# Keys and queries of the first unit: from the evicted tiles to their score buffers on chip, and the second weights asked for two tiles later

## The chip, the cores and the metric

One core of a Trainium2 chip. The metric is the device time of the whole kernel in microseconds (us), the median over several executions. Profiles are of single executions; times inside them are us from the span's start.

## The reference

Two attention blocks share one input x (2048 x 448, 16 heads of 28) and are mixed by a gate per row. A looks at 8 keys, two rows apart, at and behind each query; B at all keys.

```python
def _B_ref(x, wqkv, wo):
    qkv = (x @ wqkv).reshape(B, S, 3, H, Dh).transpose(2, 0, 3, 1, 4)
    q, k, v = qkv[0], qkv[1], qkv[2]
    scores = einsum("bhqd,bhkd->bhqk", q, k) * (Dh ** -0.5)
    o = einsum("bhqk,bhkd->bhqd", softmax(scores), v)
    return o.transpose(0, 2, 1, 3).reshape(B, S, D) @ wo
...
g = sigmoid((x * gate_w).sum(-1, keepdims=True))
return g * _A_ref(x, A_wqkv, A_wo) + (1 - g) * _B_ref(x, B_wqkv, B_wo)
```

## The kernel before

The kernel works in three stages. The first, up to about 259 us, projects x to the queries and keys (Q, K) and values of B and A. The second runs B's attention in 16 units of four heads (a group, four groups) and 512 queries, beside A's attention on GpSimd. The third multiplies by the output weights. To keep float32 accuracy on products of rounded operands, an operand is split into a high part (a rounding copy, on ScalarE, ACT) and a low part (a subtraction, on VectorE, DVE, or GpSimd, POOL), and a product is the sum of three.

Everything here is in the first stage. Its loop (from line 449 on: `for n, t in enumerate(tiles)`) goes over output tiles n; a Q or K tile is 128 rows (four heads and a bit) by 512 columns (a block nb of four). The first tiles in order are, as block and part: 0: K block 0; 1: Q block 0; 2: the third part of block 0; 3: K block 1; 4 and 5: block 1's others; 6: K block 2; 7: K block 3; 8 to 11: the rest of the first weight set. From tile 12 on the second weight set is used. The scores of unit 0 read the K rows of group 0 (`rows[0][0] == D` in the change) and the Q rows of block 0.

Order of one round n (the engines run their instructions in the order in which they are written): loads of weights that are due (`load_w`, line 244), the split of weights that are due (`split_w`, line 267: for the second set two quarters at n = 8 and two at n = 9; copies on ACT in line 212, subtractions on POOL in line 213), the split of an x block (at n = 0, 3, 5), the tile's products on TensorE (PE), then `qk_tile` (line 337). That evicts the tile from PSUM: for n < 10 (`FULL`) a copy on ACT into `hi` (line 341) and a subtraction on DVE into `lo` (line 342), and `qk_store` (line 329) puts both into the DRAM tensors qk_hi and qk_lo. `hi` and `lo` of one tile are the halves of one buffer of a pool of eight (`pp`). Whole tiles use the PSUM buffers PS[n % 4]; from n = 10 on (`project_halves`, line 308) each tile is computed in two halves of the contraction at a time, in PJ = PS[0:2], with 21 products a tile, and is summed on POOL.

From tile 11 on (`S1_START`) score products of the first pass, which finds the maxima, are mixed in between: four a tile (`s1_half`, line 153; the product itself is line 143 in `s1_mm`), which read a K block kc from KH[0] and 128 columns of QP[0]. KH[i] holds the four heads of a group at partitions 0, 32, 64 and 96, 28 rows each. QP[i] is a pair of buffers with every second head, and zeros in the other rows.

All loads and stores of this stage but the first x block's go through the queue of SyncE (SP), which issues them in the order written; a transfer that has to wait holds those behind it. `dma_r` (line 100) issues one transfer and stands for all of KH's, QP's and the stores'; `load_w` issues lines 256 (raw, three quarters of the contraction, two column ranges for the second set) and 218 (wt, the tail, twice, for each of two ranges). `load_k` (line 103) reads a group's K back from qk_hi in four transfers, one a head, `load_qhi` (line 130) a unit's Q. Before the loop SP has issued the first weights and all of x.

In before, the loop's end issues the second weights behind tiles 2 (raw) and 3 (tail), Q of unit 0 behind tile 3, and K of group 0 in two column ranges behind tiles 7 and 8.

Of the kernel before, what the change touches and what calls it, by code (L numbers as in the profile page):

```python
# [15 lines left out]
S, D, H, DH = 2048, 448, 16, 28  # L16
# [9 lines left out]
def gated_mix_kernel(ctx: ExitStack, tc: tile.TileContext, xT, xn, gw, wA, wB, woAB, out):  # L26
# [4 lines left out]
    qk_hi = dram.tile([2 * D, S], F32R, name="qk_hi")  # L31
# [40 lines left out]
    KH = [cp.tile([128, S], F32R, name=f"KH{i}") for i in range(2)]  # L72
# [5 lines left out]
    QP = [[cp.tile([128, 512], F32R, name=f"QP{i}{k}") for k in range(2)] for i in range(2)]  # L78
# [6 lines left out]
    def pair(name):  # L85
        return pp.tile([128, 2, 512], F32, tag="P", name=name)
# [3 lines left out]
    def ptile(name):  # L90
        if name[0] == "w":
            return pair(name)[:, 0, :]
        h = half.setdefault(name[:2], [])
        if not h:
            t = pair(name)
            h.extend((t[:, 1, :], t[:, 0, :]))
        return h.pop()

    def dma_r(dst, src):
        nc.sync.dma_start(dst.bitcast(F32), src.bitcast(F32))  # L100


    def load_k(g, t, src, c=slice(0, S)):
        for h in range(4):
            r = D + 112 * g + DH * h
            dma_r(t[32 * h:32 * h + DH, c], src[r:r + DH, c])
# [18 lines left out]
    qhis = {}  # L125
# [4 lines left out]
    def load_qhi(u):  # L130
        g, b = divmod(u, NB)
        qhis[u] = QP[u % 2]
        for h in range(4):
            r = 112 * g + DH * h
            dma_r(qhis[u][h % 2][32 * h:32 * h + DH, :], qk_hi[r:r + DH, 512 * b:512 * b + 512])
# [46 lines left out]
    def max_turn(t):  # L182
        r = sp.tile([128, 32], F32, name="nms")
        nc.vector.transpose(r, t)
        return r
# [18 lines left out]
    with tc.tile_pool(name="xp", bufs=1) as xp, tc.tile_pool(name="wp", bufs=2) as wp:  # L204
# [3 lines left out]
        def raw3():  # L208
            return wp.tile([128, 3, 450], F32, tag="raw", name="raw", bufs=2)
# [6 lines left out]
        def both(dst, src, eng=nc.sync):  # L216
            for h in (0, 64):
                eng.dma_start(dst[h:h + 64], src)
# [25 lines left out]
        def load_w(wi, tails=(False, True)):  # L244
            src, cols = WSRC[wi]
            if wi not in wraw:
                wraw[wi] = raw3(), wp.tile([128, 450], F32, tag="wt", name="wt"), sum(c1 - c0 for c0, c1 in cols) + 2 * (wi == GATE)
            r, t, _ = wraw[wi]
            for tail in tails:
                o = 0  # L250
                for c0, c1 in cols:
                    e = o + c1 - c0
                    if tail:
                        both(t[:, o:e], src[384:448, c0:c1])
                    else:
                        nc.sync.dma_start(r[:, :, o:e], src[0:384, c0:c1].rearrange("(k p) c -> p k c", p=128))
                    o = e

                if wi == GATE:
                    if tail:  # L260
                        both(t[:, o:o + 2], gw[0:2, 384:448].rearrange("i p -> p i"))
                    else:
                        for kt in range(3):
                            nc.sync.dma_start(r[:, kt, o:o + 2],
                                              gw[0:2, 128 * kt:128 * kt + 128].rearrange("i p -> p i"))

        def split_w(wi, kts):
            if wi not in wsets:
                wsets[wi] = [wp.tile([128, 4, 450], F32R, tag=g, name=f"{g}{wi}") for g in ("wh", "wl")]
            wh, wl = wsets[wi]  # L270
            r, t, n = wraw[wi]
            for kt in kts:
                split(wh[:, kt, :n], wl[:, kt, :n], r[:, kt, :n] if kt < 3 else t[:, :n], nc.gpsimd)
# [55 lines left out]
        def qk_store(nb, rows, hi, lo):  # L329
            cs = slice(512 * nb, 512 * nb + 512)  # L330
            for dst, t in ((qk_hi, hi), (qk_lo, lo)):
                o = 0
                for r0, r1 in rows:
                    dma_r(dst[r0:r1, cs], t[o:o + r1 - r0])
                    o += r1 - r0

        def qk_tile(n, nb, rows):
            hi, lo = ptile("qkh").bitcast(F32R), ptile("qkl").bitcast(F32R)
            if n < FULL:
                bank = PS[n % 4][:, 0, :]  # L340
                nc.scalar.activation(hi, bank, AF.Copy)
                nc.vector.tensor_tensor(out=lo, in0=bank, in1=hi.bitcast(F32), op=ALU.subtract)
                qk_store(nb, rows, hi, lo)
                return
            raw = pair("raw")
            nc.scalar.activation(raw, PJ[n % 2], AF.Copy)
            r = raw[:, 0, :]
            nc.gpsimd.tensor_tensor(out=r, in0=r, in1=raw[:, 1, :], op=ALU.add)

            def finish():  # L350
                nc.scalar.activation(hi, r, AF.Copy)
                nc.gpsimd.tensor_tensor(out=lo, in0=r, in1=hi.bitcast(F32), op=ALU.subtract)
                qk_store(nb, rows, hi, lo)

            fini.append((n + 1, finish))
# [52 lines left out]
        r, t = xst[:, 0, 0:3, :], xst[:, 0, 3, :]  # L408
# [16 lines left out]
        def split_third():  # L425
            c = slice(256, 384)
            for kt in range(3):
                split(wh0[:, kt, c], wl0[:, kt, c], wr1[:, kt, 128:256])
            split(wh0[:, 3, c], wl0[:, 3, c], wt0[:, c])
# [19 lines left out]
        for n, t in enumerate(tiles):  # L449
            wi = t[0]  # L450
            for w in loads:
                if loads[w] == n:
                    load_w(w)
            for w in splits:
                i, k = (n - splits[w][0]) * splits[w][1], splits[w][1]
                if 0 <= i < 4:
                    split_w(w, range(i, i + k))
            if n == 0:
                split_third()
            if n in (3, 5):  # L460
                split_x((n + 1) // 2)
            if n < FULL:
                project(n)
            else:
                project_halves(n, [S1_START <= m < S1_START + 80 for m in (n, n + 1)])
            if t[1] == "qk":
                qk_tile(n, t[2], t[3])
            elif t[1] == "v":
                add_halves(n, V[:, t[2], :, 0:DH])
            else:  # L470
                a_tile(n, t[2], t[3])
            if n == 0:
                split_x(1)
            while fini and fini[0][0] <= n:
                fini.pop(0)[1]()
            if n in (2, 3):
                load_w(1, (n == 3,))
            if n == 3:
                load_qhi(0)
            if n == 7:  # L480
                load_k(0, KH[0], qk_hi, slice(0, 1536))
            if n == 8:
                load_k(0, KH[0], qk_hi, slice(1536, S))
            if n == 16:
                for i in (1, 2):
                    nc.sync.dma_start(a_scr[i][:, 0:NJ, :].rearrange("c j e -> c (j e)").rearrange(
                        "c (a b) -> c a b", b=NJ), omg[0:8, None, :].to_broadcast([8, 56, NJ]))
            if n == 32:
                nc.gpsimd.memset(V[:, :, :, DH:], 1.0)
            if n == 22:  # L490
                load_k(1, KH[1], qk_hi)
            if n == 62:
                load_k(0, KL[0], qk_lo)
            if parts and parts[0][0] <= n:
                _, u, t = parts.pop(0)
                max_store(u, max_turn(t.bitcast(F32)))
            if finished and n < len(tiles) - 3:
                u = finished.pop(0)
                parts.append((n + 3, u, max_parts(u)))
            if n == 64:  # L500
                gate = []
                for sgn, dst in ((-1.0, g_t), (1.0, omg)):
                    e = sp.tile([128, NJ], F32, name="ez")
                    nc.scalar.activation(e, zt, AF.Exp, scale=sgn)
                    nc.gpsimd.tensor_tensor(out=e, in0=e, in1=V[:, 0, :, DH], op=ALU.add)
                    gate.append((dst, e))
            if n in (66, 68):
                nc.vector.reciprocal(*gate.pop(0))
            if n == 70:
                r = max_turn(omw)  # L510
                for a in range(4):
                    nc.sync.dma_start(og_scr.rearrange("(j p) -> j p", j=NJ)[:, 32 * a:32 * a + 32],
                                      r[32 * a:32 * a + NJ, :])
            if n == 76:
                load_q(0)
# [167 lines left out]
    for c in range(8):  # L683
# [20 lines left out]
        n = 0  # L704
# [197 lines left out]
    for u in range(NU - 1):  # L902
        f = NJ * (u + 1)
# [239 lines left out]
```

## Time and profile before

| | |
|---|---|
| median of 3 executions | 927.08 us (926.46 to 927.43) |
| the profiled execution | 927.55 us |
| its span, first to last instruction | 925.1 us |
| mean granted clock of TensorE | 0.996 |
| PE, DVE, ACT, POOL busy | 914.6, 732.6, 652.8, 620.9 us |

The page lists busy times by engine over the whole span. For a change of a few lines at the beginning, the answers of the trace for the first 60 us are what is to be read: what each engine did in order of time, what it waited for, and the clock that PE was granted. Transfers are listed by the time that SP took to issue them, which is not the time that they took to land. A granted clock of 1.00 is 2.4 GHz, of 0.50 is 1.2 GHz.

### The profile page before, as it was taken

The numbers are of one execution on the slowest core, as the hardware profiler recorded it, in microseconds if no ns is written. First come the engines' busy times: TensorE is split into PE (matmuls) and PEld (weight loads), VectorE is DVE, ScalarE is ACT, GpSimd is POOL, SyncE is SP. The second block draws the span as 40 slices with busy tenths as digits, with TensorE's granted clock in tenths as the row PEclk, the third lists the DMA queues.
The fourth block names the chain that finished last, engine by engine and source line by source line (L and its number), as shares of the span: only waits on it lengthen the run. The fifth ranks groups of instructions, "written<-read, shape, count | busy, mean of one in ns | idle before, by whom it ended". The sixth has DMA issues, their size and how long they took to land.

```text
span 925.1 us, 21392 instructions
## 1 busy us (share of the span) xinstructions
PE 914.6 (99%) x8396; PEld 541.3 (59%) x8396; DVE 732.6 (79%) x977; ACT 652.8 (71%) x802; POOL 620.9 (67%) x485
## 2 busy tenths in 40 slices
PE   9899999999999999999999999999999999999998
PEld 6688999999954444444444444444444444466667
DVE  6388999999979999999999999999998888500012
ACT  6346534343378888888888888888989889855551
POOL 2289856464469799999999999999994851300100
PEclk9899999999999999999999999999999999999999
DMA  9867603444362341335135232421412123553422
GB/s 254 283 191 219 185 11 82 130 121 128 104 240 64 99 123 46 88 103 130 41 96 151 85 101 63 139 74 30 107 42 53 33 60 99 149 156 112 137 83 98
DMA packets 101124, 104.34 MB, mean 113 GB/s; under 512 B 61652, under 2 KB 71252, under 8 KB 100240
## 3 DMA queue, kind: packets, MB, share of 16 engines
q1 hardware_dynamic: 100880, 102.72, 39.2%
q8 instruction: 65, 1.06, 0.5%
q10 hardware_dynamic: 144, 0.26, 0.2%
q14 instruction: 35, 0.29, 0.1%
HBM read 61.99 MB, written 40.48 MB: 111 GB/s over the span
## 4 chain that ended last, share of the span: by engine, by line
PE 94%; DMA 2%; ACT 1%; SPq 1%; issue 0%; DVE 0%; POOL 0%; ACTq 0%; DVEq 0%; POOLq 0%
PE T L1011 30%; PE av L973 26%; PE r L296 15%; PE T L812 8%; PE r L291 7%; PE r L143 4%; PE T L143 4%; ACT P L1014 1%; PE T L790 1%; DMA V<-in_xT 1%; DMA onlo<-on_lo 1%; DMA qk_hi<-qkh 0%; DMA KH<-qk_hi 0%; SPq L100 0%; SPq L851 0%
## 5 line engine op out<-in xcount | busy, mean ns | idle before, releaser
L1014 ACT ACTIVATE P<-T 128x1024 f32<-128x1024 f32 x512 | 497.1, 1024 | 89.5 <-PE T L1011 87.6
L147 DVE TENSOR_REDUCE MX<-T 128x1 f32<-128x512 f32 x470 | 443.4, 954 | 39.6 <-PE T L143 15.7
L973 PE MATMUL av<-P,V 128*32 128x512 f32 x2048 | 272.8, 605 | 0.0
L1011 PEld LDWEIGHTS T<-QH,KH 30*128 30x128 f32 x1024 | 90.9, 181 | 228.9 <-ACT P L1014 198.5
L143 PE MATMUL T<-KH,QP 28*128 28x512 f32 x704 | 222.0, 461 | 0.1
L1011 PE MATMUL T<-QH,KH 30*128 30x512 f32 x1024 | 220.6, 491 | 1.4 <-ACT P L1014 1.3
L160 DVE TENSOR_REDUCE MX<-r 128x2 f32<-128x1024 f32 x160 | 192.5, 1221 | 29.4 <-PE r L143 24.7
L1011 PE MATMUL T<-QH,KL 28*128 28x512 f32 x1024 | 189.0, 393 | 0.0
L1011 PE MATMUL T<-QL,KH 28*128 28x512 f32 x1024 | 187.4, 392 | 0.0
L608 POOL TENSOR_TENSOR prod<-qt,kt 128x896 f32<-128x896 f32 x64 | 135.1, 2115 | 4.7 <-DMA kt<-a_scr 4.7
L360 ACT ACTIVATE raw<-r 128x896 f32<-128x896 f32 (+1 forms) x64 | 58.9, 921 | 96.7 <-PE r L296 96.7
L663 POOL TENSOR_TENSOR oat<-oat,prod 128x896 f32<-128x896 f32 x56 | 118.1, 2109 | 2.4
L143 PE MATMUL r<-KH,QP 64*128 64x512 f32 x320 | 99.4, 395 | 3.3 <-DMA KH<-qk_hi 3.2
L143 PEld LDWEIGHTS T<-KH,QP 28*128 28x128 f32 x704 | 86.0, 181 | 23.7 <-ACT P L1014 13.9
L658 POOL TENSOR_TENSOR prod<-vt,L 128x896 f32<-128x896 f32 x56 | 95.5, 1705 | 0.5
L361 POOL TENSOR_TENSOR ast<-raw 128x448 f32<-128x448 f32 x48 | 55.5, 1156 | 57.8 <-ACT raw L360 49.2
L1011 PEld LDWEIGHTS T<-QL,KH 28*128 28x128 f32 x1024 | 92.5, 184 | 0.0
L1011 PEld LDWEIGHTS T<-QH,KL 28*128 28x128 f32 x1024 | 91.8, 183 | 0.9
L296 PE MATMUL r<-wh,xh 64*128 64x448 f32 (+1 forms) x512 | 87.8, 363 | 0.0
L973 PEld LDWEIGHTS av<-P,V 128*32 128x32 f32 x2048 | 40.3, 108 | 78.9 <-issue 73.9
L800 DVE TENSOR_TENSOR oalo<-T,oah 128x384 fp32r<-128x384 f32 x16 | 8.9, 557 | 90.9 <-ACT onhi L799 82.3
L296 PE MATMUL r<-wh,xl 64*128 64x448 f32 (+1 forms) x384 | 70.9, 363 | 0.0
(110 smaller groups left out, 1158.5 us busy)
## 6 DMA issues: line engine op xcount, KB each, us to landing
a_scr<-ast SPq DMA_DIRECT2D x24, 448.0 KB
qk_hi<-qkh SPq DMA_DIRECT2D x24, 256.0 KB
qk_lo<-qkh SPq DMA_DIRECT2D x24, 256.0 KB
rbc<-rs SPq DMA_DIRECT2D x60, 64.0 KB
QP<-qk_hi SPq DMA_DIRECT2D x64, 56.0 KB
KL<-qk_lo SPq DMA_DIRECT2D x16, 224.0 KB
QH<-qk_hi SPq DMA_DIRECT2D x64, 56.0 KB
QL<-qk_lo SPq DMA_DIRECT2D x64, 56.0 KB
```

The lines of the kernel that those rows point to most:

```text
L143: nc.tensor.matmul(bank, qhis[u][h % 2][r, 128 * qs:128 * qs + 128], KH[u // NB % 3][r, 512 * kc:512 * kc + 512], start=True, stop=True)
L147: nc.vector.tensor_reduce(MX[:, n % NMX:n % NMX + k], bank, axis=X, op=ALU.max)
L160: nc.vector.tensor_reduce(m, PM[k], axis=X, op=ALU.max)
L291: nc.tensor.matmul(bank, ws[c][rows, k, t[4]:t[4] + 128], x, start=first, stop=last)
L296: nc.tensor.matmul(bank[:, 0:cols], x, ws[c][rows, k, 0:cols], start=first, stop=last)
L608: nc.gpsimd.tensor_tensor(out=p, in0=qt[c], in1=kvt["k", c % 2][:, HALO - DIL * w:HALO - DIL * w + NJ, :], op=ALU.mult)
L658: nc.gpsimd.tensor_tensor(out=dst.rearrange("p j (h d) -> p j h d", d=DH), in0=kvt["v", c % 2][:, HALO - DIL * w:HALO - DIL * w + NJ, :].r ...
L663: nc.gpsimd.tensor_tensor(out=oat[c], in0=oat[c], in1=oat[c, w], op=ALU.add)
L812: writes(bank, nc.tensor.matmul(bank[:, :D], src, wo[c][:, k, :], start=(first and k == ks[0] and i == 0), stop=(last and k == ks[-1] and ...
L973: nc.tensor.matmul(av[32 * h:32 * h + 32, :], V[:, kt, 4 * g + h, :], tiles_[h], start=(kt == 0), stop=(kt == NJ - 1), skip_group_check=True)
L1011: nc.tensor.matmul(bank[a], (KH[g % 3], KH[g % 3], KL[g % 2])[t][r, ks], (qh, ql, qh)[t][r, :], start=(t == 0), stop=(t == 2))
L1014: nc.scalar.activation(p, RP[0] if a == "2" else mine, AF.Exp, scale=SCALE)
```

## The change

When a K tile of group 0 (tiles 0, 3, 6, 7) has been copied to `hi` on ACT, SP issues four transfers, one a head, from `hi` straight into KH[0], ahead of the tile's two stores. Likewise four into QP[0] for the Q tile of block 0 (tile 1). The loads of KH[0] (group 0) and QP[0] (unit 0) from qk_hi are gone; everything is still stored into qk_hi and qk_lo. The second weights are asked for behind tiles 4 and 5 instead of 2 and 3; their splits stay at tiles 8 and 9.

```diff
@@ qk_tile
             if n < FULL:
                 bank = PS[n % 4][:, 0, :]
                 nc.scalar.activation(hi, bank, AF.Copy)
+                for h in range(4):
+                    r, f = slice(32 * h, 32 * h + DH), slice(DH * h, DH * h + DH)
+                    if rows[0][0] == D:
+                        dma_r(KH[0][r, 512 * nb:512 * nb + 512], hi[f])
+                    elif rows[0][0] == 0 and nb == 0:
+                        dma_r(QP[0][h % 2][r], hi[f])
                 nc.vector.tensor_tensor(out=lo, in0=bank, in1=hi.bitcast(F32), op=ALU.subtract)
                 qk_store(nb, rows, hi, lo)
                 return
@@ the loop over tiles
-            if n in (2, 3):
-                load_w(1, (n == 3,))
+            if n in (4, 5):
+                load_w(1, (n == 5,))
             if n == 3:
-                load_qhi(0)
-            if n == 7:
-                load_k(0, KH[0], qk_hi, slice(0, 1536))
-            if n == 8:
-                load_k(0, KH[0], qk_hi, slice(1536, S))
+                qhis[0] = QP[0]
```

## Rows read from the trace of the kernel before

**Rows 1.** The page: span, and part 1, each engine's busy time, share, instructions.

```profile
span 925.1 us, 21392 instructions
...
PE 914.6 (99%) x8396; PEld 541.3 (59%) x8396; DVE 732.6 (79%) x977; ACT 652.8 (71%) x802; POOL 620.9 (67%) x485
```

**Rows 2.** Chain of waits, 0 to 130 us: start, duration, what the chain ran through.

```profile
9.86 21.22 PE r L291 x90
...
32.33 4.03 DMA qk_hi<-qkh
...
36.79 3.77 DMA KH<-qk_hi
```

**Rows 3.** PE in order of time: start, duration, operation, idle time before and its releaser.

```profile
33.54 1.20 PE L291 MATMUL r<-xh,wh 64*128 64x512 f32 x8
...
37.10 0.41 PE L291 MATMUL r<-xh,wl 64*128 64x512 f32 x2
40.70 0.76 PE L143 MATMUL r<-KH,QP 64*128 64x512 f32 x1 [3.18 <-DMA KH<-qk_hi]
...
41.97 0.76 PE L143 MATMUL r<-KH,QP 64*128 64x512 f32 x1
```

**Rows 4.** Busy time by stretch: PE, PEld, DVE, ACT, POOL (x instructions), granted clock, DMA, GB/s.

```profile
37.50:40.00 2.50, 0.01 (x1) 0.00 (x0) 0.00 (x0) 0.00 (x0) 1.26 (x1) 1.00 0.87 225
40.00:46.80 6.80, 6.02 (x26) 4.63 (x27) 2.64 (x3) 1.48 (x2) 0.37 (x1) 0.50 0.73 235
46.80:60.00 13.20, 13.20 (x116) 10.84 (x114) 10.72 (x9) 6.25 (x9) 11.00 (x9) 1.00 0.53 180
```

**Rows 5.** SP's queue in order of time, 0 to 60 us: start, duration, line, transfer.

```profile
18.23 0.32 SPq L100 DMA_DIRECT2D qk_hi<-qkh  x1
...
20.71 2.08 SPq L256 DMA_DIRECT2D raw<-in_wB  x2
...
28.34 2.00 SPq L100 DMA_DIRECT2D QP<-qk_hi  x4
30.45 0.35 SPq L100 DMA_DIRECT2D qk_hi<-qkh  x1
30.89 0.38 SPq L100 DMA_DIRECT2D qk_lo<-qkh  x1
...
32.33 0.76 SPq L100 DMA_DIRECT2D qk_hi<-qkh  x1
...
36.41 2.31 SPq L100 DMA_DIRECT2D KH<-qk_hi  x4
...
49.85 1.17 SPq L218 DMA_DIRECT2D wt<-in_wB  x2
```

**Rows 6.** Line 100's transfers: duration min/median/max in ns, first and last start.

```profile
L100 SPq DMA_DIRECT2D onhi<-onhi x4: 746/770/881, 908.6 to 911.2; - x4
L100 SPq DMA_DIRECT2D onlo<-onlo x4: 746/747/754, 912.0 to 914.4; - x4
```

**Rows 7.** SP's queue in order of time, 895 to 925 us.

```profile
908.60 3.32 SPq L100 DMA_DIRECT2D onhi<-onhi  x4
912.01 3.13 SPq L100 DMA_DIRECT2D onlo<-onlo  x4
```

**Rows 8.** ACT in order of time, 9 to 42 us.

```profile
18.19 1.68 ACT L212 ACTIVATE xh<-V 128x512 fp32r<-128x512 f32 x3 [1.74 <-DMA V<-in_xT]
...
22.41 1.68 ACT L212 ACTIVATE xh<-V 128x512 fp32r<-128x512 f32 x3
...
29.12 0.93 ACT L212 ACTIVATE wh<-raw 128x384 fp32r<-128x384 f32 x2
31.11 0.60 ACT L341 ACTIVATE qkh<-r 128x512 fp32r<-128x512 f32 x1 [1.06 <-PE r L291]
```

**Rows 9.** SP's waits, 0 to 60 us: who waited for what, us, times, longest.

```profile
SPq L256 <- DMA V<-in_xT: 2.1, 2, 1.3
```

**Rows 10.** DVE in order of time, 27 to 47 us.

```profile
31.73 0.69 DVE L342 TENSOR_TENSOR qkh<-r,qkh 128x512 fp32r<-128x512 f32 x1 [1.79 <-DMA QP<-qk_hi]
```

**Rows 11.** Busy time by stretch, 31.5 to 37 us (columns as in rows 4).

```profile
31.50:37.00 5.50, 5.50 (x40) 4.32 (x40) 1.38 (x2) 2.24 (x5) 2.09 (x3) 1.00 1.01 364
```

## The prediction

> **What bounds the kernel now.** I first read the page's head and engine shares: PE is busy 99% of a 925.1 us span [rows 1], so only microseconds in which PE stands still, or runs at the lower clock, can be won. Then I followed the chain of waits through the first 130 us, because every line that the change touches runs there. From 9.86 us on it is PE for 21 us, then it leaves PE: a store of a tile into qk_hi that takes 4.03 us to land, and a KH load that takes 3.77 us [rows 2]. Third, PE's own order of time: the last product of tile 11 that runs before the score product begins at 37.10, the first score product waits 3.18 us for KH and starts at 40.70, and the next one, which reads the other two heads, starts at 41.97 [rows 3]. Fourth, stretches of that time: PE has nothing in 37.5 to 40.0, its granted clock in 40.0 to 46.8 is 0.50, which is the lower of its two levels (1.2 instead of 2.4 GHz), and from 46.8 on PE is busy without a gap at full clock [rows 4]. So the hole costs 3.18 us of waiting, and then 40.70 to 46.80, 6.10 us at half speed, half of which, 3.05 us, is lost. Together that is 6.23 us; behind it nothing but PE sets the time, so what is won or lost here reaches the end undiminished.
>
> **What is removed.** The KH load of group 0 (8 transfers) and Q's first load (4), both read back from qk_hi, and with them the wait for the stores to land. In before, KH is issued at 36.41, behind the stores of tiles 4 to 7 and the landing of the one at 32.33 [rows 2, 5]. In after, KH's piece nb 0 is asked for as soon as tile 0 is evicted, and the four score products of tile 11 read only that piece (kc 0); tiles 12, 13 and 14 read kc 1, 2, 3. That the waits go by piece and not by whole tile is seen in before: two separate starts, 40.70 and 41.97, one for each pair of heads [rows 3]. So the 3.18 us wait goes: gain 3.18 us, and 3.05 us of clock with it, if nothing else is late. What is late next is the question.
>
> **What is added, and where it queues.** Twenty transfers from SBUF to SBUF of 28 rows x 512: four each after tiles 0, 3, 6, 7 (KH) and 1 (QP), each ahead of that tile's two stores on SP. The trace has eight transfers of just this shape, at the end of the kernel: issuing one takes SP 0.75 to 0.88 us [rows 6], and the first four take from 908.60 to 912.01, which with the gaps is 0.85 us apiece [rows 7]; a store of a whole tile takes 0.35, one every 0.46 us (30.45, 30.89) [rows 5]. So SP, not the 16 DMA engines, pays: 20 x 0.85 = 17 us, against 12 transfers that go.
>
> When does SP run? In before it can't run ahead of the transfers: the store at 18.23 starts when x's third block has landed (ACT gets it at 18.19), though they share no tile [rows 5, 8], and SP's wait list puts 2.1 us of the second weights' load down to the x loads [rows 9]. Counting places in SP's order, each waits for the transfer eight places ahead of it. The last x load is followed in after by KH x4, two stores and QP x4, so the eighth behind it is QP's second piece. The last x load has landed by 22.4 us, when ACT splits it without a wait [rows 8].
>
> From there SP is the bound. Ahead of the second weights in after stand three QP pieces, four stores (tiles 1, 2), four KH pieces and four stores (tiles 3, 4), since the weights are now asked for behind tile 4 and not behind tile 2: 22.4 + 7 x 0.85 + 8 x 0.46 = 32.0 us, against 20.71. If a piece costs SP only what a store costs, 0.46, it is 29.3; if 0.97 (the slowest of the eight, 0.88, and the gap), 32.9. I take 32.0, from the rows of the same shape. The landing: in before, four stores from 30.45 and a fifth transfer behind them, issued at 32.33, landed at 36.36, some 4.0 us after its issue [rows 2, 5]. The same pattern (four stores, then the weights) gives 32.0 + 4.0 = 36.0 us (33.3 to 36.9).
>
> **Who waits for that.** ACT meets the split of the second weights before it evicts tile 8 (split_w stands ahead of project and qk_tile in the loop). Queued behind the waiting split on ACT are tile 8's eviction, the splits for tile 9, tile 9's eviction and tile 10's. PE's tile 10 writes PS[0], which tile 8 holds. In before the split ran at 29.12 without a wait and tile 8 was evicted at 31.11 [rows 8]; PE began tile 10 at 33.54 [rows 3]. In after: two splits 0.93, the eviction 0.60 [rows 8], DVE's subtraction 0.69 [rows 10], 2.2 us in all behind the landing, so tile 10 begins at 38.2: 4.7 us later (bounds 2.0 to 5.6). The four loads of tails take 0.59 us of SP each (the pair at 49.85 [rows 5]), come later still and hold tile 9's eviction to some 39.5, but tile 11 needs that bank only after tile 10's 21 products, 2.4 us at the 116 matmuls in 13.2 us of [rows 4]: covered at either clock. KH's last piece is issued by about 44 and lands two us later, while tile 14 comes no sooner than 38.2 + 2.4 + 3 x 2.85 = 49.2: covered by 3 us, and if it were not, its lateness would add one for one. The later stores only keep buffers of the eight-deep pool, whose next users come a tile or more behind; I cost them at nothing.
>
> **The clock.** In before it had fallen within 2.5 us of PE's going idle [rows 3, 4]. A hole of some 5 us, up to 38.2, should drop it too. The loss then: 3.05 us by the row; but there PE waited a second time, until 41.97, and counted from that end the slow stretch is 4.8 us, a loss of 2.4. I take 2.4, since after has one hole, and keep 3.05 for the range.
>
> **Sum.** -3.18 - 3.05 + 4.66 + 2.4 = +0.8 us. The profiled execution took 927.55 us (span 925.1 and 2.4 around it), 0.5 above the median of 927.08; I add the difference to the median: 927.9. This case's own range is 927.0 (tile 10 at 37.4) to 929.5 (+5.6, +3.05). The hole moves from tile 11 to tile 10 and changes its cause, from the way by DRAM to weights that are late.
>
> **Rivals.**
> 1. Bytes decide, not SP's issue: the pieces cost SP little and the weights land when the bytes ahead of them have moved. From 22.4 us: ten stores, three groups of four pieces and the weights, 10 x 0.26 + 3 x 0.23 + 0.59 = 3.9 MB at the 364 GB/s of [rows 11], 10.7 us, lands 33.1 us, tile 10 at 35.3, 1.8 us late, a hole too short to drop the clock: -6.23 + 1.8 = -4.4, 922.7 (925.1 if the clock falls after all). For it: SP's DRAM pieces take less, 2.00 us for four [rows 5]. Against it: the eight rows of the very shape. Chance 0.20. The Trainium skill has it as a rule: "DMA: Bandwidth & Descriptors", section "Issuing engines are not separate DMA queues", says that the sequencer's time to start a transfer is usually small beside the transfer itself. By that rule this rival would hold; the trace differs for 56 KB pieces, 0.75 us each to issue.
> 2. Slower: SP's issue of a piece grows while its rings are full, as a store's did (0.76 at 32.33 [rows 5]). At 0.97 apiece the weights land at 36.9, tile 10 begins at 39.1, and the clock costs its full 3.05: -6.23 + 5.6 + 3.05 = +2.4, 929.5. It decides from the point at which the weights land later than 36.4 us with the full clock loss. Chance 0.20.
> 3. The change doesn't do what it says: the first score product waits for all of KH after all. Then PE stands until about 46 us instead of 40.7: +5, 932. The two starts of [rows 3] speak against it: 0.04.
>
> **How the numbers follow.** Forecast 0.52, rivals 0.20, 0.20, 0.04, and 0.04 for the rest, split evenly. A measurement of this kernel can tell about 0.2%, 1.9 us, from no change. Faster is rival 1: 0.21; same is the forecast: 0.54; slower is rivals 2 and 3: 0.25. The range reaches from a little below rival 1's time, 922.2, past rival 2, to 930.2; it leaves out the far half of rival 1 (0.1), rival 3 and the tail of the slow side.
>
> **What would show it.** Right: SP's SBUF-to-SBUF pieces at 0.75 us or more, the first weight transfer near 32 us, ACT's split waiting for a DMA into raw until about 36, PE idle before a product of tile 10 (line 291) and not before line 143, and a granted clock of 0.50 after it. Wrong: weights landing before 33, PE idle under 2 us and the clock at 1.00 throughout; or a wait of line 143 on KH.

## The result and the profile after

| | before | after |
|---|---|---|
| median, measured side by side, 8 executions each | 927.48 us | 930.35 us |
| range | 926.46 to 929.9 | 929.06 to 931.32 |
| ratio to before, 95% interval | | 1.0027 [1.0016, 1.0038] |
| span of the profiled execution | 925.1 us | 927.9 us |
| its mean granted clock | 0.996 | 0.996 |

The changed kernel is 2.9 us slower by the medians, 0.27% by the ratio. The wait for KH is gone, and a longer one stands in its place. PE's order of time in after, where [rows 3] had the wait at 40.70 before line 143:

```profile
40.78 2.08 PE L291 MATMUL r<-xh,wh 64*128 64x512 f32 x8 [7.05 <-DVE qkh L348]
...
44.88 0.39 PE L291 MATMUL r<-xh,wh 64*128 64x512 f32 x1
...
46.26 0.62 PE L143 MATMUL r<-KH,QP 64*128 64x512 f32 x2
```

Tile 10's first product (line 291) waits 7.05 us for DVE's subtraction of an earlier tile, that is for a PSUM buffer to come free. The first score products of tile 11, at 46.26, wait for nothing. PE's matmuls take 0.39 us again from 44.88 on. The stretches, with columns as in [rows 4]:

```profile
22.00:27.00 5.00, 5.00 (x23) 4.07 (x22) 4.40 (x8) 3.41 (x7) 0.00 (x0) 1.00 0.29 83
...
33.60:40.80 7.20, 0.15 (x3) 0.02 (x2) 0.69 (x1) 1.83 (x4) 1.62 (x2) 0.78 0.91 271
40.80:44.90 4.10, 4.10 (x22) 3.26 (x24) 0.69 (x1) 1.01 (x2) 2.15 (x3) 0.55 0.58 186
44.90:60.00 15.10, 15.10 (x133) 12.68 (x131) 11.52 (x10) 7.27 (x10) 10.90 (x9) 1.00 0.81 266
```

PE is busy for 0.15 us from 33.6 to 40.8, and runs at the lower clock for the better part of 40.8 to 44.9. The first line is for later: from 22 to 27 the DMA engines are busy to 29% and move 83 GB/s.

Why tile 10 waits is on ACT (its line numbers up to 344 are those of before):

```profile
22.93 1.67 ACT L212 ACTIVATE xh<-V 128x512 fp32r<-128x512 f32 x3 [0.80 <-DMA V<-in_xT]
...
28.75 0.60 ACT L341 ACTIVATE qkh<-r 128x512 fp32r<-128x512 f32 x1 [2.00 <-PE r L291]
38.58 0.94 ACT L212 ACTIVATE wh<-raw 128x384 fp32r<-128x384 f32 x2 [9.24 <-DMA raw<-in_wB]
39.42 0.58 ACT L341 ACTIVATE qkh<-r 128x512 fp32r<-128x512 f32 x1
...
41.06 0.52 ACT L212 ACTIVATE wh<-wt 128x384 fp32r<-128x384 f32 x1 [0.64 <-DMA wt<-in_wB]
```

Tile 7 is evicted at 28.75. Then ACT stands for 9.24 us at the split of the second weights, "DMA raw<-in_wB"; in before the same split ran at 29.12 without a wait [rows 8]. Tile 8 is evicted behind it, at 39.42, and DVE frees the buffer at 40.7. The tails come in time to cost little (0.64 us more on ACT at 41.06). And why the weights are late is on SP, whose rows of before are [rows 5]:

```profile
11.96 3.68 SPq L100 DMA_DIRECT2D KH<-qkh  x4
18.53 0.37 SPq L100 DMA_DIRECT2D qk_hi<-qkh  x1
...
20.57 5.40 SPq L100 DMA_DIRECT2D QP<-qkh  x4
...
28.11 3.19 SPq L100 DMA_DIRECT2D KH<-qkh  x4
31.34 0.53 SPq L100 DMA_DIRECT2D qk_hi<-qkh  x1
...
32.93 0.41 SPq L100 DMA_DIRECT2D qk_lo<-qkh  x1
33.39 1.33 SPq L256 DMA_DIRECT2D raw<-in_wB  x2
...
35.90 2.81 SPq L218 DMA_DIRECT2D wt<-in_wB  x4
...
43.22 3.20 SPq L100 DMA_DIRECT2D KH<-qkh  x4
```

Each group of four pieces takes SP more than 3 us, those at 11.96 and 20.57 longer still, since they meet x loads that have not landed. The second weights are asked for at 33.39; in before it was 20.71.

### The profile page after: what moved, and what is told of

Same layout as the page of the kernel before. It is cut to its first block, busy times and chain, and to the rows that moved or that the text cites. A ratio compares the mean times of both kernels' runs of the same rounds, so it can differ in the third digit from the quotient of the medians.

```text
span 927.9 us, 21417 instructions
## 1 busy us (share of the span) xinstructions
PE 913.2 (98%) x8396; PEld 534.7 (58%) x8396; DVE 732.0 (79%) x977; ACT 652.4 (70%) x802; POOL 620.4 (67%) x485
## 4 chain that ended last, share of the span: by engine, by line
PE 92%; DMA 3%; SPq 2%; ACT 1%; DVE 1%; issue 0%; POOL 0%; ACTq 0%; DVEq 0%; POOLq 0%
PE T L1013 30%; PE av L975 26%; PE r L296 15%; PE T L814 8%; PE r L291 5%; PE r L143 4%; PE T L143 4%; DMA V<-in_xT 2%; SPq L100 1%; ACT P L1016 1%; PE T L792 1%; DMA onlo<-on_lo 1%; DMA wt<-in_wB 0%; SPq L218 0%; SPq L853 0%
## 5 line engine op out<-in xcount | busy, mean ns | idle before, releaser
L296 PE MATMUL r<-wh,xh 64*128 64x448 f32 (+1 forms) x512 | 82.1, 362 | 0.0
L143 PE MATMUL r<-KH,QP 64*128 64x512 f32 x320 | 80.3, 390 | 0.0
```

The lines of the kernel that those rows point to most:

```text
L143: nc.tensor.matmul(bank, qhis[u][h % 2][r, 128 * qs:128 * qs + 128], KH[u // NB % 3][r, 512 * kc:512 * kc + 512], start=True, stop=True)
L296: nc.tensor.matmul(bank[:, 0:cols], x, ws[c][rows, k, 0:cols], start=first, stop=last)
```

## The experiments

The theory: SP issues in order, the pieces cost it some 0.8 us each, and with the later place of the weights in the order they land too late for ACT. The rivals: the later place alone does it (A), the pieces alone (B), pieces do harm elsewhere too (C), it is their movement on the DMA engines and not their issue (D). All comparisons are with the kernel before on the same chip.

**One part at a time: pieces, with the weights where they were.**

```diff
-            if n in (4, 5):
-                load_w(1, (n == 5,))
+            if n in (2, 3):
+                load_w(1, (n == 3,))
```

> The changed kernel with the second weights asked for behind tiles 2 and 3 again, as in the kernel before; the twenty SBUF-to-SBUF pieces stay. Theory (SP's queue: pieces and the later place of the weights both make them late): raw is issued near 28 us, ahead of KH's second four pieces, lands some 5 us later, tile 10 begins near 35.4 instead of 40.8; the tails come behind tile 3's four pieces, near 33.7 to 36.5, land near 38.6 and hold tile 11 until some 40.4, a second hole of about 2.5 us. Against the kernel before: -6.2 + 1.9 + 2.6 = -1.7 us if the clock holds, up to +0.7 if it falls. Rival A (only the later place of the weights matters): no hole at tile 10 or 11, -6 us. Rival B (only the pieces matter): as the changed kernel, +3 us.

Measured: 925.74 us against 926.80, ratio 0.9987 [0.9975, 0.9998], within the expected -1.7 to +0.7 us. ACT's two waits and PE's two holes:

```profile
33.44 0.94 ACT L212 ACTIVATE wh<-raw 128x384 fp32r<-128x384 f32 x2 [4.21 <-DMA raw<-in_wB]
...
36.94 0.53 ACT L212 ACTIVATE wh<-wt 128x384 fp32r<-128x384 f32 x1 [1.67 <-DMA wt<-in_wB]
```

```profile
35.63 1.19 PE L291 MATMUL r<-xh,wh 64*128 64x512 f32 x8 [2.02 <-DVE qkh L348]
...
38.73 0.50 PE L291 MATMUL r<-xh,wh 64*128 64x512 f32 x1 [0.50 <-DVE qkh L348]
```

The weights land at 33.4 (some 33 was expected), the tails at 36.9 (38.6 was expected), and PE has two holes, of 2.0 and 0.5 us in its own rows. The clock of this execution stays at 1.000. It took 923.56 us and is one of two among twelve that kept the clock; the other ten have mean clocks of 0.996 to 0.998, and no trace shows where they lost it. The holes explain this execution, then, and not the whole of the median. Rival A is out all the same, since the pieces alone hold ACT's split for 4.21 us, and rival B too, since the later place adds the rest: from 0.9987 to 1.0027 is 0.4%, 3.7 us.

**The other part alone: the kernel before, with the weights asked for two tiles later.**

```diff
-            if n in (2, 3):
-                load_w(1, (n == 3,))
+            if n in (4, 5):
+                load_w(1, (n == 5,))
```

> The kernel before with the second weights asked for behind tiles 4 and 5 and nothing else changed; K and Q go by DRAM. Theory: without pieces SP gets to the weights near 27.6 us, they land near 32, tile 10 begins 0 to 1.7 us late; KH is issued where it was and PE still waits for it near 37 to 41: 0 to +2 us against the kernel before. Rival A (the later place alone makes the weights late): the split waits until 36 or later, a hole at tile 10 as in the changed kernel, and then the KH wait as well or merged with it: +3 us or more. Rival B (only the pieces matter): 0.

Measured: 924.78 us, ratio 0.9978 [0.9967, 0.9988]: faster, which neither the theory nor a rival had said. PE's waits, and its stretches:

```profile
35.14 1.20 PE L291 MATMUL r<-xh,wh 64*128 64x512 f32 x8 [1.40 <-DVE qkh L342]
...
40.57 0.47 PE L143 MATMUL r<-KH,QP 64*128 64x512 f32 x1 [1.46 <-DMA KH<-qk_hi]
...
42.28 0.47 PE L143 MATMUL r<-KH,QP 64*128 64x512 f32 x1 [1.01 <-DMA KH<-qk_hi]
```

```profile
34.00:38.00 4.00, 2.86 (x24) 2.43 (x26) 1.38 (x2) 1.80 (x5) 3.32 (x4) 1.00 1.07 324
38.00:42.00 4.00, 1.81 (x13) 0.89 (x9) 0.00 (x0) 1.01 (x1) 1.26 (x1) 1.00 0.81 230
42.00:46.00 4.00, 3.72 (x30) 3.55 (x32) 3.22 (x3) 1.55 (x2) 0.72 (x1) 1.00 0.76 260
```

The weights are somewhat late (1.40 us before tile 10), as expected, and KH is late as before (1.46 and 1.01 us). PE's waits add up to 3.87 us, more than the 3.18 us of [rows 3]. But they lie in several holes, with work in between, and the granted clock is 1.00 throughout, where [rows 4] had 0.50 for 6.8 us. By the rows, 6.23 us of hole and clock against 3.87 us of holes is a gain of 2.4; 2.0 was measured. Lateness of the weights, in this dose, broke up the hole that dropped the clock: KH comes at 40.57 as it did at 40.70 in [rows 3], but PE runs out of other work at 39.1 and not at 37.5. The other executions bear it out, as far as a mean tells: these twelve have mean clocks of 0.997 to 1.000, the 35 of the kernel before beside them 0.994 to 1.000, with only one at 1.000.

**The weights ahead of everything.** `load_w(1)` stands once behind the last x load, and not in the loop.

```diff
+        load_w(1)
         for n, t in enumerate(tiles):
...
-            if n in (4, 5):
-                load_w(1, (n == 5,))
```

> The changed kernel with the second weights asked for right behind the last x load, ahead of every tile's pieces and stores. Theory (the weights' landing is the whole of the loss): they land by 27 us, ACT's split doesn't wait, PE has neither the hole at tile 10 nor the KH wait, the granted clock stays 1.00: -6.2 us against the kernel before, 9 us against the changed kernel. Rival C (the pieces cost elsewhere too: buffers of the pool held by them, DMA engines, later stores): a wait remains between 30 and 50 us, and the gain is under 3 us.

Measured: 924.28 us, ratio 0.9971 [0.9958, 0.9983], a gain of 2.7 us and not of 6.2. ACT's split doesn't wait (it runs at 29.07). But PE waits now for the pieces themselves, and SP shows why:

```profile
43.76 0.59 PE L143 MATMUL r<-KH,QP 64*128 64x512 f32 x2 [1.20 <-DMA KH<-qkh]
...
48.06 0.47 PE L143 MATMUL r<-KH,QP 64*128 64x512 f32 x1 [0.93 <-DMA KH<-qkh]
```

```profile
39.04 3.19 SPq L100 DMA_DIRECT2D KH<-qkh  x4
...
43.38 3.19 SPq L100 DMA_DIRECT2D KH<-qkh  x4
```

With PE no longer held up at tile 10, tiles 13 and 14 come at 43 and 48, and the pieces of tiles 6 and 7 are issued at 39.04 and 43.38. In the changed kernel the 7 us hole covered them. PE is busy for 5.86 of the 8 us from 42 to 50, so the rows give -6.2 + 2.1 = -4.1 us; the rest to -2.7 is open, but for what the last section says of the clock at the first stage's end. So the theory as tested, that the weights' landing is the whole of the loss, falls: SP has more to issue than there is time for, and what stands ahead only chooses what is late. Rival C held in this form: the pieces cost where they queue, whatever they are queued behind.

**Fewer pieces.** As the last, but only tiles 0 and 1 go on chip; blocks 1 to 3 of KH come by DRAM behind tiles 7 and 8 as in before.

```diff
-                    if rows[0][0] == D:
+                    if rows[0][0] == D and nb == 0:
...
+            if n == 7:
+                load_k(0, KH[0], qk_hi, slice(512, 1536))
+            if n == 8:
+                load_k(0, KH[0], qk_hi, slice(1536, S))
```

> As the kernel with the weights ahead of all pieces, but only the pieces of tile 0 (KH, block 0) and of tile 1 (QP) go on chip, eight in all; blocks 1 to 3 of KH are loaded from DRAM behind tiles 7 and 8 as in the kernel before. Theory: tile 11 needs block 0 alone, blocks 1 to 3 are needed 3, 6 and 9 us later and come by DRAM near 40: equal to the other kernel with early weights if its loads are in time (-6.2 us), or later by what tile 12 has to wait. Rival C (the pieces cost elsewhere): faster than that kernel by more than 1 us.

Measured: 927.58 us, ratio 1.0010 [0.9999, 1.0020]. PE waits a tile later than in before, and longer:

```profile
44.26 0.76 PE L143 MATMUL r<-KH,QP 64*128 64x512 f32 x1 [4.41 <-DMA KH<-qk_hi]
```

The loads from DRAM stand behind the stores of eight tiles in SP's order, wait there 1.8 us for one of these stores to land, and are issued at 41.23; the clock falls again. The expectation had left open what tile 12 would wait; it is 4.41 us, and with the clock it eats the whole gain. Rival C doesn't show here: twelve pieces fewer are no gain when their data comes later still.

**The pieces on another queue, and nothing else changed.** The four pieces of a tile are issued by GpSimd (POOL), which in before has no work between 7 and 29 us.

```diff
-                        dma_r(KH[0][r, 512 * nb:512 * nb + 512], hi[f])
+                        nc.gpsimd.dma_start(KH[0][r, 512 * nb:512 * nb + 512].bitcast(F32), hi[f].bitcast(F32))
...
-                        dma_r(QP[0][h % 2][r], hi[f])
+                        nc.gpsimd.dma_start(QP[0][h % 2][r].bitcast(F32), hi[f].bitcast(F32))
```

> The changed kernel with one difference: the twenty SBUF-to-SBUF pieces are issued from GpSimd's queue instead of SP's; the second weights stay behind tiles 4 and 5. GpSimd has nothing to do between 6 and 29 us. Theory (the pieces' issue time on SP makes the weights late): raw is asked for near 27 us, as in the kernel before with late weights, lands near 32, tile 10 begins about 1.5 us late, no wait for KH, clock 1.00: -4.5 us against the kernel before, some 7.5 us better than the changed kernel. Rival D (not the issue but the moving of the pieces, on the DMA engines, makes the weights late): the weights land near 38 again and the time stays at +3 us. Rival E (GpSimd issues slowly and waits in order): the pieces of tiles 6 and 7 land late, or its splits and sums start late: holes at tiles 12 to 14, between -3 and +3 us.

Measured: 923.61 us against 927.33, ratio 0.9961 [0.9948, 0.9975]. The same bytes, the same places of the weights in SP's order, and the weights land 5.5 us earlier than in after. SP's rows, ACT's, PE's, and the pieces' own:

```profile
24.13 0.32 SPq L100 DMA_DIRECT2D qk_hi<-qkh  x1
...
25.41 1.50 SPq L256 DMA_DIRECT2D raw<-in_wB  x2
```

```profile
33.09 0.94 ACT L212 ACTIVATE wh<-raw 128x384 fp32r<-128x384 f32 x2 [3.67 <-DMA raw<-in_wB]
```

```profile
35.29 1.20 PE L291 MATMUL r<-xh,wh 64*128 64x512 f32 x8 [1.49 <-DVE qkh L348]
...
38.35 0.49 PE L291 MATMUL r<-xh,wh 64*128 64x512 f32 x1 [0.47 <-DVE qkh L348]
```

```profile
L345 POOL DMA_DIRECT2D KH<-qkh x16: 505/505/704, 12.0 to 31.2; - x16
...
DMA to landing us min/median/max: 4.9/5.8/7.4
```

```profile
25.41:33.09 7.68, 7.68 (x34) 6.04 (x33) 3.02 (x5) 1.82 (x5) 3.99 (x8) 1.00 1.04 374
```

SP asks for the weights at 25.41, not at 33.39; ACT's split runs at 33.09, not at 38.58; PE waits 1.49 us at tile 10 (1.5 was expected) and 0.47 at tile 11. The pieces take GpSimd half a microsecond each to issue and land some 6 us later, which no tile minds. This is the run that tells issue from movement: rival D is out. Of the 8.0 us by which SP is earlier, 6.3 are the issue of the seven pieces that stood behind the last x load in after; the rest is stores that, with no pieces ahead of them in the order, go out before that load has landed. But asking 8.0 us earlier brings the weights only 5.5 us earlier: the last line above is the time from their issue to their landing, and in it the DMA engines are busy throughout (1.04, 374 GB/s). The gain is 3.6 us by the ratio, against 4.5 expected; in this execution the clock falls once more, at the end of the first stage (0.76 on the mean of 255 to 262 us).

**The pieces on GpSimd's queue and the weights where they were.** Both edits above.

> The pieces on GpSimd's queue and the second weights behind tiles 2 and 3. Theory: SP does what it did before, less twelve loads, so the split of the weights doesn't wait at 29 us and no wait for KH is left: -6.2 us against the kernel before, with the clock at 1.00 up to 256 us. Rival E (GpSimd issues slowly): holes at tiles 12 to 14 by late pieces, above -4 us.

Measured: 921.22 us against 927.33, ratio 0.9929 [0.9909, 0.9949]: 6.6 us faster than the kernel before, and by the two ratios some 9 us faster than the changed one. One of PE's rows, one of ACT's, and stretches:

```profile
28.38 0.50 PE L291 MATMUL r<-xh,wh 128*128 128x512 f32 x1 [0.99 <-DVE xh L240]
```

```profile
32.73 0.94 ACT L212 ACTIVATE wh<-raw 128x384 fp32r<-128x384 f32 x2 [1.54 <-DMA raw<-in_wB]
```

```profile
8.00:40.00 32.00, 30.61 (x148) 23.51 (x148) 17.52 (x34) 17.18 (x36) 14.57 (x25) 1.00 1.01 302
40.00:60.00 20.00, 20.00 (x175) 18.41 (x173) 17.32 (x15) 10.48 (x14) 16.17 (x14) 1.00 0.67 219
```

The score products wait for nothing and the clock is 1.00. PE's remaining waits are those of x (0.99 us at 28.38). The weights land at 32.7, not by 29: an expectation missed without a price. SP asks for them at 22.48, 2.9 us sooner than in the last run, and they land 0.4 us sooner, with the DMA engines busy all the time (1.01 from 8 to 40): by these rows it is the bytes that the weights wait for once the issue is out of the way. This is the fastest version found.

**The pieces on ACT's queue, and the weights where they were.**

```diff
-                        dma_r(KH[0][r, 512 * nb:512 * nb + 512], hi[f])
+                        nc.scalar.dma_start(KH[0][r, 512 * nb:512 * nb + 512].bitcast(F32), hi[f].bitcast(F32))
```

(and the same for QP.)

> The pieces on ACT's own queue, right behind the copy that makes them, and the second weights behind tiles 2 and 3. Issuing costs ACT some 0.76 us a piece, 3 us a tile, between 11 and 32 us, where ACT is busy some 60%: if the four PSUM buffers cover it, -6.2 us as from GpSimd's queue; if not, ACT's copies for tiles 6 to 9 and the splits come late by up to 3 us and PE waits at tile 8 to 10: between -5 and 0 us against the kernel before.

Measured: 932.78 us against 927.33, ratio 1.0063 [1.0041, 1.0084], outside of the expected -5 to 0. ACT's rows, one of PE's, and the stretches:

```profile
28.75 3.33 ACTq L345 DMA_DIRECT2D KH<-qkh  x4
32.12 0.60 ACT L341 ACTIVATE qkh<-r 128x512 fp32r<-128x512 f32 x1 [3.41 <-DMA KH<-qkh]
32.61 1.66 ACT L212 ACTIVATE xh<-V 128x512 fp32r<-128x512 f32 x3
```

```profile
33.29 1.83 PE L291 MATMUL r<-xh,wh 128*128 128x512 f32 x3 [1.84 <-ACT xh L212]
```

```profile
30.00:36.00 6.00, 3.33 (x11) 1.61 (x9) 3.25 (x6) 3.65 (x7) 0.00 (x0) 0.86 0.69 227
36.00:46.00 10.00, 9.49 (x30) 7.21 (x30) 2.42 (x4) 2.75 (x6) 1.54 (x2) 0.74 0.75 252
```

A tile's four pieces hold ACT for 3.33 us, and what stands behind them on ACT comes late: evictions, and the splits of x. PE is busy for 3.33 of the 6 us from 30 to 36, and the clock falls. The expectation asked whether the four PSUM buffers cover the late evictions. They nearly do: PE waits 1.5 us in all for a buffer, but 5.2 us for the splits of x, which the next tile needs at once (here tile 7, at 33.29).

## Why the prediction was right or wrong

The mechanism was right at each step that it named but one, the landing of the weights: no wait for KH is left; SP is the bound up to the weights and not the DMA engines (29% busy from 22 to 27 in after, 86% from 27 to 31, while SP's rows follow each other with pauses of some 0.1 us); the split of the second weights holds ACT; tile 10 is late; the clock falls. "The hole moves from tile 11 to tile 10 and changes its cause" is what the profile shows. The size of the likeliest case was wrong: it said no change, 0.8 us slower, with a range of its own to 929.5, and the kernel is 2.9 us slower. Against the median of before on which it was made, 930.35 lies just outside the stated range's upper end, 930.2; against the median measured beside it, the change of 2.9 us lies inside the range's 3.1. That the range reaches so far is luck: the likeliest case's own ended at 929.5, and the rest was put there for rival 2, whose mechanism did not come. (That case's lower end, 927.0 for tile 10 at 37.4, comes to 927.1 by the same sum.) Two terms of the sum were too small, both in one direction.

**SP's time up to the weights**: 32.0 us forecast, 33.39 measured. The price of a piece was right:

```profile
L100 SPq DMA_DIRECT2D KH<-qkh x16: 746/760/971, 12.0 to 45.7; - x16
...
L100 SPq DMA_DIRECT2D QP<-qkh x4: 747/772/1432, 20.6 to 25.2; - x4
```

Medians of 0.76 and 0.77 us, as in [rows 6]. What was missed is that the last x load landed later (ACT waits for it until 22.93, not 22.4), that one QP piece took 1.43 us, and that stores behind pieces cost 0.5 us each and not 0.46. The place in the order is borne out by SP's wait list of after, in which the pieces and stores of line 100, which share no tile with x, wait for x loads, and by QP's second piece, which starts at 22.93 with ACT's last split of x:

```profile
SPq L100 <- DMA V<-in_xT: 5.9, 5, 2.9
```

**The landing of the weights**: 4.0 us after their issue forecast, 5.2 measured (33.39 to 38.58). The row that I took it from [rows 2, 5] was a fifth store of 256 KB. The weights are 576 KB, so the row was of the wrong size; four stores and the weights are 1.6 MB, and from 33.6 to 40.8 the engines moved 271 GB/s at a busy share of 0.91. I had the rate for this, 364 GB/s [rows 11], and used it only for rival 1. Here the bytes did count, behind the issue; that is read from these rows, and no run changed the bytes alone.

With tile 10 at 40.78 instead of 38.2, and the lower clock from 40.78 to 44.88, the forecast's own sum gives -3.18 - 3.05 + 7.24 + 2.05 = +3.1 us; the spans differ by 2.8.

**The clock's term** was forecast at 2.4 and came to 2.05 here. That it is a term at all was right for the changed kernel in each of its executions: their mean clock is 0.993 to 0.996. For the kernel before, the 3.05 us are the loss of the usual execution, not of all: beside the runs with GpSimd's queue its executions go from 923.73 us at 1.000 to 929.71 at 0.994. The mean clock also shows by what the variants win. The few executions of before that kept a mean clock of 1.000 (three of the 52 beside the experiments) took 923.73 to 924.4 us. At that clock, the late weights alone took 923.42 to 925.51, the weights first 923.67 to 925.0. By these few executions, of which no trace of before was kept, almost all that these two variants gain is that the clock falls less often. GpSimd's queue with the weights early took 919.98 to 921.45 at that clock, and so is faster in itself.

**The rivals.** 1 (bytes alone decide) was wrong for this kernel, as the run with GpSimd's queue shows: with the pieces off SP the same bytes land 5.5 us earlier. In that run its sum is met, since there the bytes do decide: 33.1 and 35.3 us were forecast for the landing and for tile 10, 33.09 and 35.29 measured (so close by luck, since the last x load landed at 23.39 and not at 22.4). The rule of the Trainium skill that it went by ("DMA: Bandwidth & Descriptors", section "Issuing engines are not separate DMA queues", that starting a transfer is usually short beside the transfer) is one that these pieces are an exception to: each takes 0.76 us of SP's time to issue, and with that time off SP the weights came earlier. 2 had nearly the right time, +2.4, by the wrong mechanism: but for one of 1.43 us the pieces weren't dearer than the eight at the end (medians 0.76 and 0.77), and no run shows how full a ring was. 3 was wrong: the score products waited for nothing.

**What I priced at nothing** deserves its own line. KH's last pieces, of tile 7, were "covered by 3 us". They were, in after, and those of tile 6 with them; the cover was the hole itself. With the weights early they became the bound at once (43.76 and 48.06 above). The kernel with nothing but late weights showed the opposite error: a wait added on purpose was priced as a loss and was a gain, because of where it fell.

## What to carry to other kernels

A transfer that is small in bytes can still take long on the queue that issues it (0.76 us for 56 KB here), and everything behind it in that queue pays: price a new transfer in its queue's time first, and look at which engine has idle time to issue it. When one wait of several is removed, price the next in line with the time that the removed wait gave it. A hole in PE costs its length and perhaps the clock as well, so the same waiting in several short holes can be cheaper than in one (as with the late weights; on ACT's queue several holes dropped the clock too).

## What the runs showed of the hardware

- A transfer of 28 rows x 512 float32 from SBUF to SBUF takes 0.76 to 0.77 us (medians) of SP's or ACT's time to issue, a store of 128 such rows to DRAM mostly 0.32 to 0.54, and the same piece issued by GpSimd 0.505, with 4.9 to 7.4 us to land (3.4 to 9.3 with the weights early).
- The granted clock fell in holes of PE of 3.18 us (before), 7.05 (after) and 4.41 (few pieces), and not with holes of 2.02 and 0.50, or of 1.40, 1.46 and 1.01 with products in between. Length alone doesn't decide: on ACT's queue it was still 1.00 from 20 to 30 us and fell after holes of 1.06 and 1.84, both shorter than the 2.02 without a fall, the second up to 33.29. What does decide was not tried.
- The kernel's executions spread by some 6 us with the mean clock between 0.994 and 1.000. In the profiled execution with the weights first the clock fell at a place that no edit touches, where the first stage ends: 0.83 on the mean of 255 to 262 us, against 1.00 there in before (the lines below, in this order). With GpSimd's queue it fell there as well, to 0.76. The longest wait of PE there is 0.57 us in each of the three. So a gain of 2 us in this kernel needs many executions to be seen.

```profile
255.00:262.00 7.00, 6.25 (x53) 2.65 (x53) 3.91 (x5) 5.12 (x7) 4.42 (x12) 0.83 0.69 193
255.00:262.00 7.00, 6.33 (x63) 5.05 (x59) 4.47 (x5) 4.11 (x5) 3.82 (x4) 1.00 0.24 68
```
